# One-row and one-column products between the full products of a Fourier contraction, and unread products at a layer boundary

## The chip, the cores and the metric

The kernel runs on one core of one Trainium2 chip. A core has a matrix engine (PE, called TensorE), a vector engine (DVE), a scalar engine (ACT), GpSimd (POOL) and a queue engine (SP) that issues most DMAs. They share an SBUF of 128 partitions, and PE writes to eight banks of PSUM, which the other engines empty. The metric is device time in microseconds, the median of the runs shown; lower is better.

## The reference

Two kinds of layer alternate, A B A B, each added to its input after a layer norm. A is a Fourier mixing of 2048 rows by 512 columns; B is causal attention over four segments with a memory carried from segment to segment. Only A is touched by the change.

```python
def _A_ref(x, dft_seq_re, dft_seq_im, dft_hid_re, dft_hid_im):
    a = jnp.einsum("bsd,ed->bse", x, dft_hid_re)
    b = jnp.einsum("bsd,ed->bse", x, dft_hid_im)
    y = jnp.einsum("ts,bse->bte", dft_seq_re, a) - jnp.einsum("ts,bse->bte", dft_seq_im, b)
    return y
...
x = A_x
x = x + _A_ref(_layernorm(x, axis=-1), ...)
x = x + _B_ref(_layernorm(x, axis=-1), B_wq, B_wk, B_wv, B_wo, B_beta)
x = x + _A_ref(_layernorm(x, axis=-1), ...)
x = x + _B_ref(_layernorm(x, axis=-1), B_wq, B_wk, B_wv, B_wo, B_beta)
```

## The kernel before

The Fourier matrices hold cosines and sines, so their rows repeat with changed signs. The kernel folds the normalised input into eighths of the 2048 rows (octants), 128 rows to a tile and `k` = 0, 1 for the two tiles of an octant, and forms sums and differences of the octants on DVE. Then it contracts over the folded rows on PE. It runs this Fourier stage twice. What follows calls them Fourier layer 1 (at the start) and Fourier layer 2 (behind the first attention layer; there the argument `late` of `place_folded` is set, and its last octant comes straight from the attention's output projection).

The contraction, `contract(ps)`, runs for two halves `ps` = 0, 1 of the output. Each fills eight `u` tiles, four to a `kind` (0 for the cosine part, 1 for the sine part), one for each 128 of the 512 hidden columns (`d`). Its steps are:

- `odd(ps, kind, k)`: for two tiles of folded rows (`re` and `B`, which the trace names `hre` and `hAB`; in layer 2 both are `hAB`), four products of 128 rows by 256 columns each, into the odd columns of `u`.
- `even(ps, kind, k)`: for the tiles `S01` and `S32` (both `hS` in the trace), two sets of four products of 128 columns. Two families of small products hang on it. **One-row products**: for kind 0, `k` = 0, second set, a product whose operands `row["x"]` and `row["c", ps]` have a single row (`rows` in the trace), 128 columns, one after each of the four. **One-column products**: for `ps` = 0, kind 1, a column that is worked out for itself, `u[:, 0:1]`, gets a product of 128 rows and one column (`cmid,hS`), and for `k` = 0 also one of one row and one column (`cmid,rows`).

For `ps` = 0 the steps run in the order odd 0, odd 1, even 0, even 1 for `k` = 0, and again for `k` = 1. For `ps` = 1 they run kind by kind. After the last step of a kind, `drain` copies the four `u` tiles out (ACT, lines 576 and 577, then DVE, lines 594 to 602) into `vf`, and `hidden(j)` multiplies these along the hidden dimension: two `yi` products, and three `yr` products of which the middle one has a single row (`rows,wrap`). The steps of `contract(1)` and the first `hidden` units are interleaved by slot numbers given to `place`.

What sets the order: every engine runs its instructions in the order in which they were issued. `place` sorts generators into numbered slots, and the code of one slot is run after the code of the one before; PE's products are kept in exactly that program order (`keep_in_program_order`), while a scheduler may move instructions of DVE, ACT and SP among themselves by priority. The engines wait for one another through semaphores. The `u`, `yi`, `yr`, `po` and most other PSUM tiles come from one pool of seven banks (`bank`); an eighth holds `u` of kind 1, `d` = 3 (and later `pv_bank`).

The DVE operations that PE waits for in these stages are `fold_re` (line 426 where `k` = 0 and the tile is the first, line 428 otherwise), `fold_im` (lines 433 and 435) and `fold_even` (lines 440 to 454). In layer 2 the last octant is taken in by lines 380 to 388, behind the attention's last `po` products. `chk` (line 736, ACT) are activations over the given Fourier matrices that test their symmetry; they lie in the free time of ACT, and their loads in SP's queue.

Of the kernel before, what the change touches and what calls it, by code (L numbers as in the profile page):

```python
# [18 lines left out]
P = 128  # L19
# [39 lines left out]
def spectral_infini_kernel(  # L59
# [14 lines left out]
    V, A, G, T = nc.vector, nc.scalar, nc.gpsimd, nc.tensor  # L74
# [6 lines left out]
    def in_order(engine, name):  # L81
        op = getattr(engine, name)

        def call(*args, **kwargs):
            return tc.keep_in_program_order(op(*args, **kwargs))  # L85

        return call

    T = SimpleNamespace(matmul=in_order(T, "matmul"), transpose=in_order(T, "transpose"))
# [30 lines left out]
    def bank(name, shape=(P, 512), dtype=F32):  # L120
        return psum.tile(list(shape), dtype, name=name, tag="bank", bufs=7)
# [197 lines left out]
    def place_folded(x_in, x_out, t0, fold_at, folds=None, late=None):  # L319
        h = {}  # L320
        cf, vf, row, mid = {}, {}, {}, {}
        rest, minus = folded.masks

        def quad(w, k):
            if w == "re" and late is not None:
                w = "A"
            if w in "AB":
                if "xT" not in h:
                    h["xT"] = sb.tile([P, 2, 2, 2, 512], F32, name="hAB", tag="xT", bufs=1)
                return h["xT"][:, k, "AB".index(w)]  # L330
            if (w, k) not in h:
                tag = "ut" if w in ("C", "D32", "re") else "wd"
                h[w, k] = pair(f"h{w}", tag, 8, F32)
            return h[w, k]
# [189 lines left out]
        def bank4(ps, kind):  # L524
            if (ps, kind) not in banks:
                banks[ps, kind] = [
                    psum.tile([P, 512], F32, name="u", tag="pv", bufs=1)
                    if (ps, kind, d) == (0, 1, DT - 1)
                    else bank(f"u{d}")
                    for d in range(DT)  # L530
                ]
            return banks[ps, kind]

        def mm(out, lhsT, rhs, start=False, stop=False):
            T.matmul(out, lhsT, rhs, start=start, stop=stop, skip_group_check=True)

        def odd(ps, kind, k):
            for n, ab in enumerate((0, 1) if late is None else (1, 0)):
                for d, u in enumerate(bank4(ps, kind)):
                    mm(  # L540
                        u.rearrange("p (x o) -> p x o", o=2)[:, :, 1],
                        quad(("re", "B")[kind], k)[:, ab, d * P : (d + 1) * P],
                        cf[ps, k][:, ab, kind * 256 : (kind + 1) * 256],
                        start=(k, n) == (0, 0),
                        stop=(k, n) == (1, 1),
                    )

        def even(ps, kind, k):
            src = quad(("S01", "S32")[kind], k)
            for n, r in enumerate((2, 0)):  # L550
                for d, u in enumerate(bank4(ps, kind)):
                    dst = u.rearrange("p (x o) -> p x o", o=4)[:, :, r]
                    at = kind * 256 + n * P
                    mm(
                        dst,
                        src[:, n, d * P : (d + 1) * P],
                        cf[ps, 2][:, k, at : at + P],
                        stop=k == 1,
                    )
                    if (kind, n, k) == (0, 1, 0):  # L560
                        mm(dst, row["x"][:, d * P : (d + 1) * P], row["c", ps])
            if (ps, kind) == (0, 1):
                src = quad("S01", k)
                for d, u in enumerate(bank4(ps, kind)):
                    cols = slice(d * P, (d + 1) * P)
                    mm(u[:, 0:1], src[:, 1, cols], row["mid"][:, k : k + 1], stop=k == 1)
                    if k == 0:
                        mm(u[:, 0:1], row["x"][:, cols], row["mid"][0:1, 2:3])

        def drain(ps, kind):  # L570
            u = banks.pop((ps, kind))
# [36 lines left out]
            for to, of in pairs:  # L608
                G.tensor_copy(f[:, kind, :, to], v[:, :, of])
                if kind == 0:  # L610
                    G.tensor_copy(w[:, to], b[0:1, of])

        def contract(ps):
            if ps == 0:
                steps = [(f, kind, k) for k in range(2) for f in (odd, even) for kind in range(2)]
            else:
                steps = [(f, kind, k) for kind in range(2) for k in range(2) for f in (odd, even)]
            for f, kind, k in steps:
                f(ps, kind, k)
                if (f, k) == (even, 1):  # L620
                    drain(ps, kind)
                yield
# [79 lines left out]
        for ps in range(2):  # L702
            for n in (0, 2, 1):
                at = t0 + 8 + n if ps else t0 - 6 + n if late is not None else t0 - 10 + 3 * n // 2
                place(3.5, load_c(ps, n), [at])
        place(2, contract(0), [t0 + k for k in (0, 2, 4, 5, 6, 8, 9, 11)])
        place(2, contract(1), [t0 + k for k in (13, 14, 17, 19, 21, 22, 23, 24)])
        place(3.5, load_w(), [t0 + 9])
        for j in range(8):
# [684 lines left out]
    else:  # L1394
# [11 lines left out]
        for t, (edge, other) in zip(folded.masks, ((0.0, 1.0), (0.0, -1.0))):  # L1406
            V.memset(t, other)
            V.memset(t[0:1], edge)
        place_folded(
            Rows(x), mids[0], a1,  # L1410
            lambda k: [a1 - 12 + 3 * k, a1 - 6 + 4 * k, a1 - 4 + 4 * k, a1 - 2 + 4 * k],
# [5 lines left out]
        )  # L1417
        e = b1 + LB
        place_folded(
            mids[1], mids[2], a2,  # L1420
            lambda k: [e - 56 + 6 * k, e - 52 + 6 * k, e - 46 + 6 * k, e - 16 + 14 * k, e - 13 + 13 * k, e - 10 + 13 * k, e + 1 + 4 * k, *((e + 11, e + 13, e + 14) if k == 0 else (e + 15, e + 15, e + 17))],
            late=taken,
# [60 lines left out]
    ident = ident_b = mask = same_head = gate = None  # L1483
# [147 lines left out]
```

## Time and profile before

| | us |
|---|---|
| median of three runs | 1254.58 |
| lowest, highest | 1246.12, 1265.04 |
| the profiled execution | 1254.79 |
| its span, first to last instruction | 1252.9 |
| PE busy in it | 1148.4 (92%) |
| DVE busy | 962.3 (77%) |
| ACT busy | 845.8 (68%) |
| POOL busy | 440.3 (35%) |
| mean granted PE clock, of 1 | 0.968 |

Fourier layer 1 lies at about 0 to 130 us of the span and Fourier layer 2 at about 600 to 750, each overlapping the attention layer next to it. A busy share is a mean over stages that have different limits; in each stage the chain of waits tells which engine the end hangs on. The granted clock is that of PE: at 0.5 the array takes half of the clock pulses. The profile's PE busy time includes weight loads that a product waits for.

### The profile page before, as it was taken

How to read it: one execution, taken by the hardware profiler on the slowest of the kernel's cores; microseconds unless marked ns; L12 is line 12 of the kernel's file. 1: busy time of each engine (PE TensorE's matmuls, PEld its weight loads, DVE VectorE, ACT ScalarE, POOL GpSimd, SP SyncE). 2: the span in 40 equal slices, each digit the busy share in tenths (PEclk: the TensorE clock that was granted, in tenths of full speed). 3: DMA queues.
4: the chain of work that ended last, by engine and by line, in shares of the span. 5: the costliest groups of instructions: out<-in, count | busy, mean ns of one | idle time of the engine just before them, and what ended most of it. 6: DMA issues, size and time to landing. Idle time of an engine off the chain costs nothing.

```text
span 1252.9 us, 24306 instructions
## 1 busy us (share of the span) xinstructions
PE 1148.4 (92%) x7590; PEld 742.4 (59%) x7590; DVE 962.3 (77%) x3565; ACT 845.8 (68%) x1902; POOL 440.3 (35%) x774
## 2 busy tenths in 40 slices
PE   2999898999999999988889898899999999999887
PEld 2877464666655665544568765556666656655454
DVE  8878977778877777777695889867787778767872
ACT  2733487887787787786525426878777887878762
POOL 1121543534444444441110234444434544435200
PEclk9889998999999999998988999999999999999999
DMA  7877543435544454372426864434454444534511
GB/s 286 278 250 240 183 131 121 148 120 166 160 149 121 139 175 139 122 220 86 165 86 225 283 214 157 147 112 125 131 170 155 135 145 141 162 129 129 163 44 54
DMA packets 111125, 197.65 MB, mean 158 GB/s; under 512 B 13917, under 2 KB 63075, under 8 KB 110986
## 3 DMA queue, kind: packets, MB, share of 16 engines
q1 hardware_dynamic: 107722, 195.22, 48.2%
q8 instruction: 62, 1.02, 0.3%
q10 hardware_dynamic: 3264, 0.79, 0.3%
q14 instruction: 77, 0.63, 0.2%
HBM read 128.04 MB, written 67.14 MB: 156 GB/s over the span
## 4 chain that ended last, share of the span: by engine, by line
PE 64%; DVE 17%; ACT 7%; issue 5%; DMA 5%; POOL 2%; ACTq 0%; SPq 0%; DVEq 0%; POOLq 0%
PE pqk L85 11%; PE pv_bank L85 9%; PE sT L85 8%; PE nat L85 8%; DVE junk L934 7%; PE u L85 6%; PE po L85 5%; PE pvv L85 5%; DMA chk<-in_chk 3%; PE yr L85 2%; ACT pT L1008 2%; PE pm L85 2%; PE pM L85 2%; PE on L85 1%; ACT sT L1007 1%
## 5 line engine op out<-in xcount | busy, mean ns | idle before, releaser
L934 DVE CUSTOM_DVE_ANT_0 junk<-nat,mask 128x512 bf16<-128x512 f32 (+3 forms) x1024 | 499.9, 488 | 146.5 <-PE nat L85 113.0
L1008 ACT ACTIVATE pT<-sT 128x512 f32<-128x512 f32 x640 | 367.4, 598 | 44.5 <-PE sT L85 19.6
L1013 POOL TENSOR_SCALAR_AFFINE_SELECT pT<-pT 128x512 f32<-128x512 f32 x392 | 170.1, 447 | 404.7 <-ACT pT L1008 366.6
L85 PE MATMUL sT<-stkq,stkk 99*128 99x256 bf16 (+3 forms) x1024 | 250.6, 308 | 11.8 <-DVE mx L934 7.2
L85 PE MATMUL nat<-stkk,stkq 96*128 96x512 bf16 (+3 forms) x1024 | 237.8, 304 | 19.1 <-DVE mx L934 17.5
L1007 ACT ACTIVATE sT<-sT 128x256 f32<-128x256 f32 (+1 forms) x560 | 182.1, 334 | 52.4 <-PE sT L85 49.0
L85 PEld LDWEIGHTS <-stkk 99*128 99x128 bf16 x1024 | 83.1, 99 | 136.5 <-issue 122.2
L85 PE MATMUL pv_bank<-pT,vt 128*17 128x512 f32 (+3 forms) x2048 | 152.9, 437 | 0.0
L85 PEld LDWEIGHTS <-stkq 96*128 96x128 bf16 x1024 | 93.0, 99 | 65.2 <-issue 29.1
L85 PE MATMUL pqk<-xT,wq 128*128 128x512 f32 x384 | 127.6, 445 | 3.1 <-ACT xT L97 2.3
L85 PE MATMUL pqk<-xT,wk 128*128 128x512 f32 x384 | 126.3, 441 | 0.7 <-DVE mx L934 0.4
L85 PE MATMUL pvv<-wv,xT 128*128 128x512 f32 x384 | 124.2, 438 | 2.1 <-DVE mx L934 2.0
L85 PE MATMUL po<-wo,oh 128*128 128x512 f32 x384 | 122.5, 437 | 2.4 <-DVE oh L99 1.6
L736 ACT ACTIVATE chk<-chk,reps 128x1024 f32<-128x1024 f32 (+1 forms) x80 | 81.5, 1021 | 57.2 <-DMA chk<-in_chk 56.2
L85 PEld LDWEIGHTS pv_bank<-pT,vt 128*17 128x17 f32 x2048 | 53.5, 98 | 81.0 <-issue 76.7
L1118 POOL TENSOR_TENSOR onat<-onat,otmp 128x128 f32<-128x128 f32 x96 | 48.7, 514 | 104.3 <-DVE otmp L1117 101.0
L934 DVE DVE_READ_ACCUMULATOR2_ANT mx<- 128x1 f32 x1024 | 84.0, 82 | 0.0
L874 POOL TENSOR_TENSOR parts<-rem,parts 128x512 bf16<-128x512 f32 x60 | 71.8, 1196 | 27.8 <-ACT parts L870 24.2
L85 PEld LDWEIGHTS po<-wo,oh 128*128 128x128 f32 x384 | 68.4, 193 | 22.0 <-DVE oh L99 4.6
L85 PEld LDWEIGHTS pqk<-xT,wq 128*128 128x128 f32 x384 | 69.8, 193 | 16.4 <-ACT xT L97 2.8
L85 PEld LDWEIGHTS pvv<-wv,xT 128*128 128x128 f32 x384 | 68.6, 192 | 15.9 <-DVE mx L934 4.4
L85 PEld LDWEIGHTS pqk<-xT,wk 128*128 128x128 f32 x384 | 68.7, 194 | 13.4 <-issue 0.9
(216 smaller groups left out, 1679.4 us busy)
## 6 DMA issues: line engine op xcount, KB each, us to landing
chk<-in_chk SPq DMA_DIRECT2D x68, 512.0 KB
stkq<-scrq SPq DMA_DIRECT2D x64, 384.0 KB
stkk<-scrk SPq DMA_DIRECT2D x64, 384.0 KB
scrq<-parts SPq DMA_DIRECT2D x32, 384.0 KB
scrk<-parts SPq DMA_DIRECT2D x32, 384.0 KB
mid<-xrm SPq DMA_DIRECT2D x32, 256.0 KB
scrq<-parts SPq DMA_DIRECT2D x32, 256.0 KB
scrk<-parts SPq DMA_DIRECT2D x32, 256.0 KB
```

Source lines behind the costliest of these rows:

```text
L85: return tc.keep_in_program_order(op(*args, **kwargs))
L736: A.activation(t[:, c : c + row], t[:, c : c + row], AF.Abs, bias=rep[:, col : col + 1], scale=scale, accum_out=acc[:, col : col + 1],)
L874: E.tensor_tensor(out=parts[:, 2], in0=rem, in1=parts[:, 1], op=ALU.subtract)
L934: V.tensor_tensor_reduce(junk[:, :n], src, mask[:, 512 - n :], 1.0, 3e38, ALU.add, ALU.min, dst,)
L1007: A.activation(blocks, blocks, AF.Relu)
L1008: A.activation(dst, ps, AF.Exp, scale=-SCALE)
L1013: G.affine_select(blocks, blocks, pattern=[[0, n] for n in blocks.shape[1:-1]] + [[1, P]], compare_op=ALU.is_ge, fill=0.0, base=0, channel ...
L1118: G.tensor_tensor(out=dst, in0=dst, in1=tmp, op=ALU.add)
```

## The change

Three things change, all in `place_folded`.

- The one-row products of both contractions, and for `ps` = 0 the one-column products of `k` = 0, are no longer issued in `even`. They go into a list, `extras`, and `odd` takes them from there for `k` = 1: for `ps` = 0 one after each of its products, for `ps` = 1 one after every second.
- The one-column products of `k` = 1 stay where they were.
- In layer 2 alone (`late is not None`), `contract(0)` first issues fifteen products of the identity with itself, 128 by 128 in four-byte data, into a PSUM tile `warm` that nobody reads.

```diff
+        extras = []
+
         def odd(ps, kind, k):
...
                         stop=(k, n) == (1, 1),
                     )
+                    if k and extras and (ps == 0 or d % 2):
+                        mm(*extras.pop(0))
...
                     if (kind, n, k) == (0, 1, 0):
-                        mm(dst, row["x"][:, d * P : (d + 1) * P], row["c", ps])
+                        extras.append((dst, row["x"][:, d * P : (d + 1) * P], row["c", ps]))
...
                     cols = slice(d * P, (d + 1) * P)
-                    mm(u[:, 0:1], src[:, 1, cols], row["mid"][:, k : k + 1], stop=k == 1)
                     if k == 0:
-                        mm(u[:, 0:1], row["x"][:, cols], row["mid"][0:1, 2:3])
+                        extras.append((u[:, 0:1], src[:, 1, cols], row["mid"][:, 0:1]))
+                        extras.append((u[:, 0:1], row["x"][:, cols], row["mid"][0:1, 2:3]))
+                    else:
+                        mm(u[:, 0:1], src[:, 1, cols], row["mid"][:, 1:2], stop=True)
...
+        def warm(n):
+
+            ps = bank("warm")
+            for _ in range(n):
+                T.matmul(ps[:, :P], ident, ident, start=True, stop=True)
+
         def contract(ps):
...
+            if ps == 0 and late is not None:
+                warm(15)
```

On PE, in Fourier layer 1, at the turn from `k` = 0 to `k` = 1 of the first contraction, this stood before (a row gives the line, the operation, out<-in and the size of the output):

```order
L85 MATMUL u_283<-cmid,hS_184 128x1
L85 MATMUL u_283<-cmid,rows 128x1
L85 MATMUL u<-cmid,hS_184 128x1
L85 MATMUL u<-cmid,rows 128x1
L85 MATMUL u_229<-cf,hre 128x256
L85 MATMUL u_230<-cf,hre 128x256
L85 MATMUL u_231<-cf,hre 128x256
```

The last three rows are the first products of `k` = 1, which wait for DVE's line 428. On the same engine, the same products of `k` = 1 now, from the third of them on:

```order
L85 MATMUL u_231<-cf,hre 128x256
L85 MATMUL u_231<-rows 128x128
L85 MATMUL u_232<-cf,hre 128x256
L85 MATMUL u_232<-rows 128x128
L85 MATMUL u_229<-cf,hre 128x256
L85 MATMUL u_281<-cmid,hS_184 128x1
L85 MATMUL u_230<-cf,hre 128x256
L85 MATMUL u_281<-cmid,rows 128x1
L85 MATMUL u_231<-cf,hre 128x256
L85 MATMUL u_282<-cmid,hS_184 128x1
```

The four one-row and eight one-column products have moved from ahead of that wait to behind it, one after each of twelve full products.

On PE, in Fourier layer 1, in the second contraction (`ps` = 1), ahead of the first `hidden` unit, this stood before:

```order
L85 MATMUL u_496<-rows 128x128
L85 MATMUL u_497<-cf,hS_184 128x128
L85 MATMUL u_497<-rows 128x128
L85 MATMUL u_498<-cf,hS_184 128x128
L85 MATMUL u_498<-rows 128x128
L85 MATMUL yi<-wf,vf 128x256 x2
```

Now, on PE, behind the second `hidden` unit:

```order
L85 MATMUL u_495<-cf,hre 128x256
L85 MATMUL u_496<-cf,hre 128x256
L85 MATMUL u_495<-rows 128x128
L85 MATMUL u_497<-cf,hre 128x256
L85 MATMUL u_498<-cf,hre 128x256
L85 MATMUL u_496<-rows 128x128
L85 MATMUL u_495<-cf,hre 128x256
```

The four one-row products have moved from between products of 128 columns to behind every second product of 256 columns, past two `hidden` units. Fourier layer 2 changes in the same way in both places.

On PE, at the boundary of the first attention layer and Fourier layer 2 (with the semaphores that a row waits for), before:

```order
L85 MATMUL po<-wo,oh 128x512 [waits DVE_49]
L85 MATMUL po<-wo,oh 128x512 x9
L85 MATMUL u_8530<-cf,hAB 128x256 [waits DMAHW7_49,DVE_49,PE_49]
L85 MATMUL u_8531<-cf,hAB 128x256 [waits PE_49]
L85 MATMUL u_8532<-cf,hAB 128x256
L85 MATMUL u_8533<-cf,hAB 128x256
L85 MATMUL u_8530<-cf,hAB 128x256 [waits DVE_49]
```

And now:

```order
L85 MATMUL po<-wo,oh 128x512 [waits DVE_49]
L85 MATMUL po<-wo,oh 128x512 x9
L85 MATMUL warm<-ident 128x128 [waits PE_49]
L85 MATMUL warm<-ident 128x128 x14
L85 MATMUL u_8546<-cf,hAB 128x256 [waits DMAHW7_49,DVE_49,PE_49]
L85 MATMUL u_8547<-cf,hAB 128x256
L85 MATMUL u_8548<-cf,hAB 128x256
L85 MATMUL u_8549<-cf,hAB 128x256 [waits PE_49]
L85 MATMUL u_8546<-cf,hAB 128x256 [waits DVE_49]
```

The fifteen unread products stand between the attention's last projection and the first `u` product, which still waits for DVE and for its DMA.

On ACT, in Fourier layer 2, where the first rows of the next attention layer are prepared, before:

```order
L736 ACTIVATE chk,acc<-chk,reps 128x1024 [waits DMAHW2_49,Activation_49]
L97 ACTIVATE xT<-xnT 128x4x128 [waits PE_49]
L97 ACTIVATE xT<-xnT 128x4x128
L577 ACTIVATE ub<-u_8913 128x512 [waits PE_49]
L97 ACTIVATE xT<-xnT 128x4x128 [waits PE_49]
L576 ACTIVATE ua<-u_8912 128x512 [waits DVE_49]
L97 ACTIVATE xT<-xnT 128x4x128 [waits PE_49]
```

And now (lines 582 and 583 are lines 576 and 577 of before, and 750 is 736):

```order
L97 ACTIVATE xT<-xnT 128x4x128 [waits PE_49]
L97 ACTIVATE xT<-xnT 128x4x128
L583 ACTIVATE ub<-u_8929 128x512 [waits PE_49]
L750 ACTIVATE chk,acc<-chk,reps 128x1024 [waits DMAHW2_49,Activation_49]
L97 ACTIVATE xT<-xnT 128x4x128 [waits PE_49] x2
L582 ACTIVATE ua<-u_8928 128x512 [waits DVE_49]
```

One check has moved from ahead of the four copies `xT` to between them, and the copy `ua` behind them.

## The prediction

> **What bounds the kernel now.** I read the page's head and its chain of work, then the chain in order of time, then PE's timeline in the two Fourier stages, and last the windows, because the clock column told where PE was slow without waiting.
>
> ```profile
> span 1252.9 us, 24306 instructions
> PE 64%; DVE 17%; ACT 7%; issue 5%; DMA 5%; POOL 2%; ACTq 0%; SPq 0%; DVEq 0%; POOLq 0%
> ...
> 43.28 21.73 PE u L85 x112
> ...
> 647.48 35.38 PE u L85 x192
> ```
>
> PE carries 64% of the chain. The last two rows (start, us, what) are the `u` products of the contractions in Fourier layer 1 (from 43.28) and Fourier layer 2 (from 647.48): both lie on the chain, so a microsecond of PE there is a microsecond of the end. The profiled execution took 1254.79 us with this span, 0.2 above the median 1254.58; I sum against 1254.79.
>
> PE's timeline follows (start, us, then the group). Products of four-byte data appear as two records, so x32 is 16 products.
>
> ```profile
> 33.42 0.48 PE L85 MATMUL u<-rows 1*128 1x128 f32 x2
> ...
> 35.91 0.48 PE L85 MATMUL u<-rows 1*128 1x128 f32 x2
> ...
> 38.22 0.28 PE L85 MATMUL u<-cmid,hS 128*128 128x1 f32 x2
> ...
> 40.29 0.38 PE L85 MATMUL u<-cmid,rows 1*128 1x1 f32 x2
> 43.28 6.33 PE L85 MATMUL u<-cf,hre 128*128 128x256 f32 x16 [2.62 <-DVE hre L428]
> ...
> 52.91 3.73 PE L85 MATMUL u<-cf,hS 128*128 128x128 f32 x32
> 56.48 0.95 PE L85 MATMUL u<-cmid,hS 128*128 128x1 f32 x8
> 57.29 3.70 PE L85 MATMUL u<-cf,hre 128*128 128x256 f32 x16
> ...
> 64.94 1.40 PE L85 MATMUL yi<-wf,vf 128*128 128x256 f32 x4
> ...
> 73.38 3.62 PE L85 MATMUL u<-cf,hre 128*128 128x256 f32 x16
> 76.83 1.03 PE L85 MATMUL yi<-wf,vf 128*128 128x256 f32 x4
> 77.70 0.59 PE L85 MATMUL yr<-wf,vf 128*128 128x256 f32 x2
> 78.22 0.69 PE L85 MATMUL yr<-rows,wrap 1*128 1x256 f32 x2
> 78.84 0.70 PE L85 MATMUL yr<-wf,vf 128*128 128x256 f32 x2
> 79.38 1.95 PE L85 MATMUL u<-cf,hS 128*128 128x128 f32 x16
> ```
>
> Prices at full clock, from starts: a 256-column product 0.431 (73.38 to 76.83, eight), a 128-column one 0.223 (52.91 to 56.48, sixteen). In the one-row stretch a product starts every 0.415 (33.42 to 35.91, six steps), though a 128-column stream is 0.223: each switch between 128 rows and one row shows a weight load of 0.19. The one-column products start every 0.296 (38.22 to 40.29, seven steps). The same switch beside 256 columns: the three `yr` products, the middle one of one row, take 1.68 (77.70 to 79.38) against 3 x 0.431, so two switches cost 0.39 there too. Long neighbours do not hide them.
>
> The windows (us, busy per engine, granted clock, DMA) stand on a grid of 3.413 us on which the clock is exactly 0.50 or 1.00:
>
> ```profile
> core 0: us, PE busy (x) PEld busy (x) DVE busy (x) ACT busy (x) POOL busy (x), PEclk, DMA share, GB/s
> 45.19:48.61 3.42, 3.42 (x10) 2.70 (x9) 3.42 (x5) 1.47 (x4) 0.00 (x0) 0.50 0.70 238
> ...
> 62.26:65.67 3.41, 3.41 (x17) 2.51 (x17) 0.48 (x1) 2.29 (x5) 0.35 (x3) 1.00 0.87 348
> 65.67:69.09 3.42, 3.42 (x8) 1.89 (x7) 1.28 (x2) 1.66 (x4) 0.00 (x0) 0.50 0.02 6
> 69.09:72.50 3.41, 3.41 (x8) 2.29 (x8) 2.55 (x5) 0.00 (x0) 0.00 (x0) 0.50 0.43 153
> ...
> 642.53:645.94 3.41, 2.38 (x6) 1.97 (x7) 3.41 (x11) 0.00 (x0) 0.30 (x1) 0.50 0.41 121
> 645.94:649.35 3.41, 3.24 (x9) 2.07 (x8) 3.41 (x5) 0.63 (x1) 1.22 (x2) 0.50 0.29 114
> ...
> 659.59:663.01 3.42, 3.42 (x23) 3.21 (x22) 3.39 (x5) 2.16 (x3) 0.00 (x0) 1.00 0.71 204
> 663.01:666.42 3.41, 3.41 (x9) 2.70 (x8) 1.12 (x2) 1.56 (x4) 0.00 (x0) 0.50 0.79 261
> 703.97:707.38 3.41, 2.15 (x10) 1.94 (x11) 3.12 (x14) 2.19 (x3) 1.04 (x2) 1.00 0.76 297
> ```
>
> The clock falls after a window with little full-row streaming, even when PE shows busy all of it. 62.26 to 65.67 is mostly one-row pairs (full-row share 0.223/0.83 = 27%; with the `yi` behind them some 42%), and 659.59 to 663.01 is mostly one-column products (some 28%): both are followed by 0.50. The window 703.97, busy 63%, is not. So the fall lies between 42 and 63%. For the way back: 642.53 (70% busy) does not release, 645.94 (95%) does; `yi` and `yr` together (4 x 0.431 of 2.55 = 68%) fail in one window and release in the next. The edge is near 70%.
>
> The Trainium skill, "TensorE: Matmul & The Clock Gate", Part 1: The HAM clock gate, says that the window is free-running and about 3.4 us, and the gate half or full; the rows above agree. The same page, Why this matters for your kernels, asks only that PE have no idle gap over about 3 us; the full window 659.59 with its fall behind it disagrees, and the measurement decides. By that rule alone nothing but idle time would move the clock, and the estimate would be +4.4 us.
>
> **The change, part by part.**
>
> *Layer 1, first contraction.* Four one-row products (0.61 each: 0.223 and two switches) and eight one-column products (0.296) ran before 40.67 and so in the shadow of PE's wait for DVE, which ends at 43.28 whatever PE does. Now they run behind it: 4 x 0.61 + 8 x 0.296 = **+4.8**. Bounds: 1.7 if their weights loaded unseen, 4.8 by the rows; I take the rows.
>
> *The clock there.* At 43.28 it is half, as before. Before, sixteen plain products filled the window 45.19 and it came back at 48.61. Now the share is 0.431/1.04 = 41% beside one-row products and 0.431/0.727 = 59% beside one-column ones, both below 70%, so it stays until the last four plain products. Half clock runs at 0.51 of full: 64.94 to 73.38 is 8.44 for what takes 2 x 2.55 = 5.10 at full, with 6.83 of it at half. The 9.98 us of interleaved work then take 19.6, to 62.9, and the next grid line is 65.67: 22.4 us at half lose 11.0. Before, 9.63 for 16 x 0.431 lost 2.7. **+8.3**; bounds 0 (release at 48.61) and 8.3. The one-column share is nearest to the windows that failed, so I take 8.3.
>
> *Layer 1, second contraction.* The one-row pairs leave the place ahead of `yi`; the clock should not fall at 65.67: 8.44 - 5.10 = **-3.3**. Their four products cost the same 0.61 in the later place, two 256-column products to each (0.862/1.47 = 59%, inside 42 to 63, so a fall is possible but not likely). `yi` also waits for DVE's `vf`; the plain products ahead of it leave that little slack, bound 0 to 0.5, taken as 0.
>
> *Layer 2, the boundary.*
>
> ```profile
> 631.31 8.74 PE L85 MATMUL po<-wo,oh 128*128 128x512 f32 x36
> 643.56 3.75 PE L85 MATMUL u<-cf,hAB 128*128 128x256 f32 x8 [3.50 <-issue]
> 647.48 6.36 PE L85 MATMUL u<-cf,hAB 128*128 128x256 f32 x24 [0.17 <-DVE hAB L426]
> 653.67 1.28 PE L85 MATMUL u<-cf,hS 128*128 128x128 f32 x10
> ...
> 662.05 8.86 PE L85 MATMUL u<-cf,hAB 128*128 128x256 f32 x32
> 670.75 3.73 PE L85 MATMUL u<-cf,hS 128*128 128x128 f32 x32
> ...
> 682.78 1.43 PE L85 MATMUL yi<-wf,vf 128*128 128x256 f32 x4
> ...
> 691.22 3.62 PE L85 MATMUL u<-cf,hAB 128*128 128x256 f32 x16
> ```
>
> Fifteen unread products take 15 x 0.223 = 3.35, and the wait is 3.50 (640.05 to 643.56): they fit, delay nothing, and keep the clock. Four products then end at 645.3, but the next four need DVE's L426, ready at 647.48: PE waits 2.2 us instead. Only the twelve after that gain: 647.48 + 12 x 0.431 = 652.66 against 653.67, **-1.0**. If that 2.2 us gap falls whole into one window its share is 35% and a window at half costs 3.41 x 0.49 = 1.7; on the present grid it is split, so 0. The unread tile takes one PSUM bank of the rotation; PE alone is waited for, so nothing.
>
> *Layer 2, contractions.* The one-column stretch no longer empties a window: 670.75 - 662.05 = 8.70 against 16 x 0.431 = 6.90, **-1.8**. The one-row pairs leave the place ahead of 682.78: again 8.44 - 5.10, **-3.3**. The moved products cost as much as before, 0.
>
> *The other queues.* ACT's order shifts: a check now stands between the copies `ub` and the last two `xT`.
>
> ```profile
> 713.09 1.15 ACT L736 ACTIVATE chk<-chk,reps 128x1024 f32<-128x1024 f32 x1
> ...
> 715.20 0.59 ACT L577 ACTIVATE ub<-u 128x512 f32<-128x512 f32 x1
> ...
> 716.98 0.60 ACT L97 ACTIVATE xT<-xnT 128x512 fp32r<-128x512 f32 x1
> ```
>
> From 715.8 a check (1.15 and its read) ends at about 717.1, two copies at 718.2 instead of 717.6: **+0.6**, and `pqk` waits for them. SP's check loads and DVE's small statistics trade places; their cover is the contraction's PE time, and I cost them at 0.
>
> Sum: 4.8 + 8.3 - 3.3 - 1.0 - 1.8 - 3.3 + 0.6 = +4.3, so 1259.
>
> **Rivals.**
> *Layer 2 falls too.* Its one-row stretch, 4 x 1.04 us at 41%, is longer than a window; what follows is at 59%. If one window catches it, about 659.6, the remaining 6.6 us of mixed work run at half until plain products fill a window, some 17 us, losing 17 x 0.49 = 8.3: 1267. For it: 41% is under 42. Against: the grid must fit.
>
> *Layer 1 recovers at 48.61.* If one-row streams count for the gate, 8.3 becomes 0 and the time is 1251. For it: the release edge rests on few windows. Against: window 62.26 streamed, one-row products counted, well over half the time and still fell.
>
> *Weights hide beside long products.* Then 0.39 vanishes for each one-row product, 1.55 in each of the four places, and some 1.5 for the one-column ones in each layer; shares rise, and the 8.3 shrinks to about 3: 4.3 - 6.2 - 3.0 - 5.3, about 1245. Against: the `yr` rows. The Trainium skill, same page, Part 2: What happens when you issue a matmul, says that a weight load is pulled ahead when row groups do not conflict or the spare weight buffer is free; by that the estimate would be this one, and the `yr` rows do not bear it out.
>
> *Slower by over 2%.* The clock stays at half through both column stages, not only the mixed stretches. 25 us need 25/0.49 = 51 us more at half, fifteen windows. Against: plain stretches such as 52.91 to 56.48 fill whole windows.
>
> *The change does not do what it says.* The unread products, whose operand is the identity, do not hold the clock: only the 1.0 is lost, 1260.
>
> **How the numbers follow.** The sum's case 0.45 (1259, the last rival within it), layer 2 falling too 0.21 (1267), early recovery 0.16 (1251), hidden weights 0.10 (1245), others 0.08. The time told is the first. The runs before lie between 1246 and 1265, so the median itself moves by several us. The range 1247 to 1268 takes in the first three and leaves out the fourth and the tails. Faster or slower counts from 2%, 25 us, about what a measurement of this kernel can tell from no change. No case but the fourth rival reaches it: faster 0.01, same 0.96, slower 0.03.
>
> **What would show it.** Right: in layer 1 PE idle from about 36 (40.67 less the 4.8 moved) to 43.28, and the clock at 0.50 over five to seven windows from there; in layer 2 fifteen `warm` products ahead of 643.5, clock 1.00 at the first `u`, a gap of about 2 us before L426's product; clock 1.00 over the first two `yi` of each layer; one-row products at 0.6 beside 256 columns. Wrong: the clock back at 1.00 by 52 in layer 1; one-row products that add 0.25 or less; a half-clock stretch over layer 2's mixed products; or the late hidden stage waiting for DVE, so that PE's gain is not handed on.

## The result, and the profile after

| | before | after |
|---|---|---|
| median, us (20 runs each) | 1253.05 | 1260.76 |
| lowest, highest | 1246.12, 1265.04 | 1256.77, 1265.59 |
| the profiled execution | 1254.79 | 1259.06 |
| its span | 1252.9 | 1257.3 |
| mean granted PE clock | 0.968 | 0.975 |

The ratio is 1.0068, with a 95% interval of 1.0057 to 1.0080: about 8.5 us slower (0.0068 x 1253), less than 2%. The forecast was 1259. The mean clock went up while the time went up, so the profile must be read by stage.

The head of the page of the changed kernel, then rows of its chain of work in order of time (start, us, what):

```profile
span 1257.3 us, 24369 instructions
PE 60%; DVE 17%; ACT 8%; DMA 7%; issue 5%; POOL 2%; ACTq 0%; SPq 0%; DVEq 0%; POOLq 0%
...
43.38 32.16 PE u L85 x128
...
653.94 31.13 PE u L85 x184
```

In layer 1 the `u` products ahead of the first `hidden` unit are 32.16 us of the chain where they were 21.73. In layer 2 they are 31.13 where they were 35.38: one stage lost, the other gained.

PE's timeline of the changed kernel in layer 1 (start, us, group, and in brackets the idle time before it and what ended it):

```profile
32.24 3.73 PE L85 MATMUL u<-cf,hS 128*128 128x128 f32 x32
43.38 1.22 PE L85 MATMUL u<-cf,hre 128*128 128x256 f32 x2 [7.40 <-DVE hre L428]
44.53 0.79 PE L85 MATMUL u<-rows 1*128 1x128 f32 x2
45.25 1.22 PE L85 MATMUL u<-cf,hre 128*128 128x256 f32 x2
...
62.66 3.17 PE L85 MATMUL u<-cf,hAB 128*128 128x256 f32 x8
65.67 3.73 PE L85 MATMUL u<-cf,hS 128*128 128x128 f32 x32
...
70.05 3.70 PE L85 MATMUL u<-cf,hre 128*128 128x256 f32 x16
...
75.37 1.03 PE L85 MATMUL yi<-wf,vf 128*128 128x256 f32 x4
...
80.47 1.03 PE L85 MATMUL u<-cf,hre 128*128 128x256 f32 x4
...
86.26 1.13 PE L85 MATMUL yi<-wf,vf 128*128 128x256 f32 x4
...
95.24 2.40 PE L85 MATMUL u<-cf,hAB 128*128 128x256 f32 x10 [0.53 <-DVE ve L144]
...
705.33 2.40 PE L85 MATMUL u<-cf,hAB 128*128 128x256 f32 x10 [1.09 <-DVE xrm L677]
```

The last row is the same place in layer 2. In the kernel before, the timeline had at these two places:

```profile
87.39 2.40 PE L85 MATMUL u<-cf,hAB 128*128 128x256 f32 x10 [2.22 <-DVE xrm L663]
...
705.23 2.40 PE L85 MATMUL u<-cf,hAB 128*128 128x256 f32 x10 [2.22 <-DVE rt L159]
```

PE now stands idle from 35.98 to 43.38, since nothing small is left to fill the wait, and then takes 22.29 us (43.38 to 65.67) for sixteen full products and twelve small ones. One pair of a full and a one-row product takes 1.87 us there. Two `hidden` units take 5.10 (75.37 to 80.47), where they took 8.44.

The windows of the same kernel on the clock's grid, three of layer 1 and two of layer 2's placed products:

```profile
44.57:47.98 3.41, 3.41 (x9) 1.96 (x8) 3.41 (x5) 1.20 (x2) 0.00 (x0) 0.50 0.50 157
61.63:65.04 3.41, 3.41 (x10) 2.44 (x9) 0.00 (x0) 0.00 (x0) 0.00 (x0) 0.50 0.00 0
65.04:68.45 3.41, 3.41 (x29) 3.33 (x28) 0.73 (x2) 1.47 (x3) 0.00 (x0) 0.99 0.47 135
...
662.37:665.79 3.42, 3.42 (x18) 2.11 (x16) 3.42 (x7) 0.38 (x1) 0.00 (x0) 1.00 0.74 283
665.79:669.20 3.41, 3.41 (x18) 2.39 (x17) 3.38 (x5) 2.11 (x4) 0.00 (x0) 1.00 0.66 223
```

In layer 1 seven windows pass at half, from about 41.15, still in PE's wait, to 65.04 (23.9 us). From 44.57 on PE shows busy all of every one of them and the clock is still 0.50. In layer 2 the same mixture, entered at full clock, stays at 1.00. The mixture did not lower the clock there; in layer 1 it failed to raise it.

PE's timeline of the changed kernel at the boundary and in layer 2:

```profile
637.76 8.75 PE L85 MATMUL po<-wo,oh 128*128 128x512 f32 x36
646.35 3.51 PE L85 MATMUL warm<-ident 128*128 128x128 f32 x30
650.01 1.97 PE L85 MATMUL u<-cf,hAB 128*128 128x256 f32 x8 [0.16 <-PE warm L85]
653.94 5.45 PE L85 MATMUL u<-cf,hAB 128*128 128x256 f32 x24 [1.96 <-DVE hAB L426]
659.22 3.73 PE L85 MATMUL u<-cf,hS 128*128 128x128 f32 x32
662.84 0.70 PE L85 MATMUL u<-cf,hAB 128*128 128x256 f32 x2
663.47 0.48 PE L85 MATMUL u<-rows 1*128 1x128 f32 x2
663.88 0.70 PE L85 MATMUL u<-cf,hAB 128*128 128x256 f32 x2
...
667.01 0.70 PE L85 MATMUL u<-cf,hAB 128*128 128x256 f32 x2
...
673.37 1.99 PE L85 MATMUL u<-cf,hAB 128*128 128x256 f32 x8
675.20 3.73 PE L85 MATMUL u<-cf,hS 128*128 128x128 f32 x32
...
684.91 1.03 PE L85 MATMUL yi<-wf,vf 128*128 128x256 f32 x4
...
690.01 1.03 PE L85 MATMUL u<-cf,hAB 128*128 128x256 f32 x4
```

The first four `u` products are quick now, and the time goes into a new wait of 1.96 for L426. A full and a one-row product take 1.04 here (662.84 to 663.88).

Set side by side, the two profiled executions show where the change's time came and went:

| the same work in both | before | after | difference |
|---|---|---|---|
| layer 1, second contraction starts | 57.29 | 70.05 | +12.8 |
| first `yi` | 64.94 | 75.37 | +10.4 |
| third `yi` | 76.83 | 86.26 | +9.4 |
| attention 1, `pqk` x11 | 101.29 | 108.78 | +7.5 |
| its last `po` x36 | 631.31 | 637.76 | +6.5 |
| layer 2, first `yi` | 682.78 | 684.91 | +2.1 |
| attention 2, `pqk` x11 | 718.36 | 718.81 | +0.5 |
| end of the span | 1252.9 | 1257.3 | +4.4 |

### The profile page after: what moved, and what is told of

It is laid out like the page before. It is cut to its first block, busy times and chain, and to the rows that moved or that the text cites. A ratio compares the mean times of both kernels' runs of the same rounds, so it can differ in the third digit from the quotient of the medians.

```text
span 1257.3 us, 24369 instructions
## 1 busy us (share of the span) xinstructions
PE 1145.7 (91%) x7620; PEld 737.9 (59%) x7620; DVE 963.3 (77%) x3565; ACT 844.3 (67%) x1902; POOL 439.6 (35%) x774
## 4 chain that ended last, share of the span: by engine, by line
PE 60%; DVE 17%; ACT 8%; DMA 7%; issue 5%; POOL 2%; ACTq 0%; SPq 0%; DVEq 0%; POOLq 0%
PE pqk L85 10%; PE pv_bank L85 9%; PE sT L85 8%; PE nat L85 7%; DVE junk L948 7%; PE u L85 7%; PE po L85 5%; PE pvv L85 5%; DMA chk<-in_chk 4%; ACT pT L1022 2%; PE pm L85 2%; PE pM L85 2%; ACT sT L1021 2%; PE on L85 2%; PE yr L85 1%
## 5 line engine op out<-in xcount | busy, mean ns | idle before, releaser
L85 PE MATMUL sT<-stkq,stkk 99*128 99x256 bf16 (+3 forms) x1024 | 248.0, 305 | 16.0 <-DVE mx L948 8.9
L85 PE MATMUL nat<-stkk,stkq 96*128 96x512 bf16 (+3 forms) x1024 | 235.2, 301 | 18.5 <-DVE mx L948 16.7
```

## The experiments

Twelve kernels were run, six to twelve times each, beside 25 to 35 runs of the kernel before on the same chip. Three questions: is the loss in layer 1 the clock or the moved products; does each other part give what the sum said; and is there a better place for the small products. Most kernels switch the parts through one function, put into the changed kernel:

```diff
+        def deferred(ps):
+            return <condition>
...
-                        extras.append((dst, row["x"][:, d * P : (d + 1) * P], row["c", ps]))
+                        one = (dst, row["x"][:, d * P : (d + 1) * P], row["c", ps])
+                        extras.append(one) if deferred(ps) else mm(*one)
```

and the same for the one-column products; with `True` it is the changed kernel. Below only the condition is given, and whether the unread products run. The results:

| kernel | median, us | ratio to before | 95% interval |
|---|---|---|---|
| l1_first | 1264.66 | 1.0088 | 1.0059 to 1.0117 |
| second | 1243.78 | 0.9921 | 0.9892 to 0.9950 |
| l2_first | 1251.33 | 0.9979 | 0.9958 to 0.9999 |
| warm_only | 1255.25 | 1.0024 | 0.9999 to 1.0050 |
| fill_l1 | 1251.98 | 1.0010 | 0.9984 to 1.0035 |
| keep_l1 | 1247.41 | 0.9973 | 0.9947 to 0.9998 |
| grouped | 1246.97 | 0.9964 | 0.9941 to 0.9987 |
| grouped_fill | 1246.33 | 0.9965 | 0.9941 to 0.9988 |
| after_nowarm | 1262.38 | 1.0067 | 1.0038 to 1.0096 |
| keep_nowarm | 1246.99 | 0.9948 | 0.9927 to 0.9969 |
| second_warm | 1247.44 | 0.9970 | 0.9948 to 0.9992 |
| grouped_nowarm | 1246.83 | 0.9947 | 0.9925 to 0.9969 |

**Only layer 1's first contraction (l1_first).**

```diff
+            return late is None and ps == 0
...
-            if ps == 0 and late is not None:
+            if ps == 0 and late is not None and False:
                 warm(15)
```

> Only layer 1's first contraction (ps = 0) interleaves its small products; the second contractions, layer 2 and the boundary are as before. Theory 1 (the small products leave the shadow of the wait for line 428, and their mixing keeps the clock at half): first contraction ends at about 70 in the span instead of 57.3, clock 0.50 from about 41 to 65, total slower by 8 to 13 us (ratio 1.006 to 1.010). Rival A (only the 4.8 us leave the shadow, the half clock being an accident of the grid): +5 us, 1.004. Rival B (the loss of the changed kernel comes from the layer boundary, from layer 2 or from the reordered checks): no change, 1.000.

Its ratio is 1.0088, 11 us (0.0088 x 1253). PE's timeline in layer 1:

```profile
43.11 1.22 PE L85 MATMUL u<-cf,hre 128*128 128x256 f32 x2 [7.40 <-DVE hre L428]
...
71.00 3.70 PE L85 MATMUL u<-cf,hre 128*128 128x256 f32 x16
...
78.65 1.13 PE L85 MATMUL yi<-wf,vf 128*128 128x256 f32 x4
...
83.85 3.62 PE L85 MATMUL u<-cf,hre 128*128 128x256 f32 x16
```

The same idle 7.40 and 27.9 us to the second contraction, against 14.0 before (43.28 to 57.29). This one edit carries the whole loss and more, as the first theory had it.

The last two rows show something else. The second contraction of this kernel has its one-row products where the kernel before has them, and yet its first two `hidden` units took 5.20 (78.65 to 83.85) and not 8.44: in this execution the clock did not fall there.

**Only the second contractions, in both layers, without the unread products (second).**

```diff
+            return ps == 1
```

> Only the one-row products of the second contractions (ps = 1), in both layers, stand behind every second 256-column product. Theory 1: clock 1.00 over the first two yi units in both layers, 8.4 us of them become 5.1, but only in executions whose grid of windows fell on the old one-row stretch; total 2 to 7 us faster (ratio 0.995 to 0.998). Rival: DVE's work on xrm paces the hidden units, so that PE's gain ends in waits: 0.999 to 1.001 with waits of PE on DVE about 3 us longer behind the units.

The ratio is 0.9921, some 10 us (by its interval 6.3 to 13.5), where the first theory had 2 to 7. PE's timeline in layer 1 and layer 2:

```profile
62.95 1.13 PE L85 MATMUL yi<-wf,vf 128*128 128x256 f32 x4 [0.36 <-POOL vf L617]
...
68.15 1.03 PE L85 MATMUL u<-cf,hre 128*128 128x256 f32 x4
...
83.25 2.40 PE L85 MATMUL u<-cf,hAB 128*128 128x256 f32 x10 [0.86 <-DVE ve L144]
...
693.04 2.40 PE L85 MATMUL u<-cf,hAB 128*128 128x256 f32 x10 [1.09 <-DVE xrm L684]
```

Two units take 5.20 in layer 1 (62.95 to 68.15) and 5.10 in layer 2 (672.61 to 677.71) in place of 8.44, as the sum said. The `vf` wait that the prediction bounded at 0.5 is 0.36. And the later wait of PE, 2.22 before, is 0.86 and 1.09: the four one-row products, moved to behind the units, now fill a part of it. The sum had not counted that.

**Only layer 2's first contraction, without the unread products (l2_first).**

```diff
+            return late is not None and ps == 0
```

> Only layer 2's first contraction interleaves its small products; no unread products. Theory 1: the one-column stretch no longer lowers the clock, 16 products of 256 columns without a half-clock window, local gain 0 to 1.8 us less 0.5 for the dearer one-column places: ratio 0.998 to 1.001. Rival: the mixed stretch lowers the clock as in layer 1: 6 to 8 us slower, 1.005 to 1.007.

Its ratio of 0.9979 is 2.6 us, at the edge of what its interval tells from nothing. The clock does not fall in its mixed stretch. Nor does it in the five other kernels that place products there (the changed kernel, fill_l1, keep_l1, after_nowarm, keep_nowarm): the rival "layer 2 falls too" did not happen in six profiled executions. In one of them its condition was met: in keep_nowarm a whole window lay in the one-row stretch (shown in the last section).

**Only the unread products (warm_only).**

```diff
+            return False
...
             if ps == 0 and late is not None:
                 warm(15)
```

> Only the fifteen unread products at the boundary. Theory 1: clock 1.00 when the first u product of layer 2 starts, then a wait of about 2 us for line 426; gain about 1 us, up to 2.7 where the clock would also have been lost in the next window: ratio 0.998 to 0.9995. Rival A: products of the identity do not hold the clock, 1.000. Rival B: they delay the first u product or a PSUM bank, 1.001 to 1.003.

The place looks as forecast, with the clock at 1.00 and a wait of 1.96 for L426, and yet the time is not shorter: 1.0024, rival B's ratio. Rival B's cause is not seen: the first `u` product starts 12.26 us behind the start of the last `po` group (631.16 to 643.42), where it was 12.25 before. This was taken up again below.

**The changed kernel, with layer 1's wait filled (fill_l1).** Forty-four products of a two-byte identity with zeros, added to `u`, run while PE waits for L428.

```diff
+        def fill(u, n):
+            for _ in range(n):
+                mm(u[:, :384], ident_b, mask[:, :384])
...
             for f, kind, k in steps:
+                if (ps, f, kind, k) == (0, odd, 0, 1) and late is None:
+                    fill(bank4(0, 0)[0], 44)
                 f(ps, kind, k)
```

> The changed kernel, and in layer 1 PE's empty wait ahead of line 428 (35.9 to 43.4 us) is filled with 44 products of the two-byte identity with zeros, 384 columns each, which add nothing to a u tile: some 7.0 us of full-row streaming, ended before the wait is. Theory 1 (the half clock, not the moved products, is the larger part of layer 1's loss): clock 1.00 at the first product behind the wait, mixed products at 1.04 and 0.8 us a pair as in layer 2, first contraction ends about 9 us earlier than in the changed kernel, total 1250 to 1256. Rival A (the switches or a wait carry the loss): 1260, as the changed kernel. Rival B (zeros do not count for the gate): clock 0.50 there and 1260.

PE's timeline, then two windows:

```profile
35.78 7.32 PE L85 MATMUL u<-mask,ident_b 128*128 128x384 bf16 x44
43.35 0.70 PE L85 MATMUL u<-cf,hre 128*128 128x256 f32 x2 [0.25 <-DVE hre L428]
...
55.72 3.73 PE L85 MATMUL u<-cf,hS 128*128 128x128 f32 x32
60.10 3.70 PE L85 MATMUL u<-cf,hre 128*128 128x256 f32 x16
```

```profile
43.35:46.76 3.41, 3.41 (x13) 2.05 (x14) 3.41 (x5) 2.44 (x4) 0.00 (x0) 1.00 0.39 103
46.76:50.18 3.42, 3.42 (x18) 2.40 (x17) 3.42 (x6) 1.45 (x3) 0.00 (x0) 1.00 0.96 383
```

This separates the two terms of layer 1. The products are the same and start at the same time; only the clock differs. They take 12.37 us (43.35 to 55.72) in place of 22.29, so half clock cost 9.9 us of this stage; the other 12.37 - 16 x 0.431 = 5.5 are the moved products. In the time of the whole kernel the ratio went from 1.0068 to 1.0010, 7.3 us, which with the intervals (some 0.0028 together, 3.5 us) is in keeping with 9.9.

**The changed kernel, with layer 1's first contraction as before and the unread products (keep_l1).**

```diff
+            return late is not None or ps == 1
```

> The changed kernel, but layer 1's first contraction leaves its small products where they were before, in the shadow of the wait for line 428. Theory 1: all of the change's loss lies there; the rest is its second-contraction part (1243.8 alone) with layer 2's first contraction and the unread products, each 0 to -2: 1240 to 1246, faster than both kernels. Rival (the unread products or layer 2's mixing cost something, as the run with the unread products alone, 1255.3, might say): 1246 to 1250.

0.9973: the harm is gone, but the gain is smaller than `second` alone had. Its 1247.4 lies in the rival's range.

**The small products grouped where they were (grouped, grouped_fill).** Nothing is placed between full products; each four one-row products run in a row behind their four 128-column products, and the one-column products are sorted by kind. The unread products stay. The second kernel also fills layer 1's wait, with 27 products.

```diff
                     if (kind, n, k) == (0, 1, 0):
-                        extras.append((dst, row["x"][:, d * P : (d + 1) * P], row["c", ps]))
+                        one = (dst, row["x"][:, d * P : (d + 1) * P], row["c", ps])
+                        group.append(one)
+            for one in group:
+                mm(*one)
```

> The kernel before with the unread products, and no interleaving: the four one-row products of a place stand in a row behind their full products, and the one-column products of full rows ahead of those of one row. Theory 1 (a switch between 128 rows and one row costs 0.19 us, and a place now has two instead of eight): each place shorter by 1.2 us, four times in all of which the first lies in layer 1's wait; the one-row stretch, 1.3 instead of 3.3 us, can no longer empty a window, so the clock stays 1.00 over the first yi units: 1241 to 1246. Rival (each one-row product pays its own weight load, whatever stands beside it): no gain from the order, 1251 to 1255.

> As the run grouped, and what is left of layer 1's wait ahead of line 428 is filled with 27 products of the two-byte identity with zeros, about 4.3 us, adding nothing to a u tile. Theory 1: clock 1.00 at 43.3 or one window earlier than 48.6, the sixteen 256-column products behind the wait take 6.9 to 8.3 instead of 9.6 us; 1.3 to 2.7 us below the run grouped. Rival (zeros do not count for the gate): equal to the run grouped.

PE's timeline of `grouped` ahead of layer 1's first unit:

```profile
62.94 1.15 PE L85 MATMUL u<-rows 1*128 1x128 f32 x8
64.02 1.13 PE L85 MATMUL yi<-wf,vf 128*128 128x256 f32 x4
...
69.22 3.62 PE L85 MATMUL u<-cf,hre 128*128 128x256 f32 x16
```

Four one-row products in a row take 1.08 from the first start to `yi` (62.94 to 64.02): 4 x 0.223 and one switch of 0.19. The other switch shows around them: the eight products ahead start at 61.06 and need 1.78 by themselves, and the two units take 5.20 where they take 5.10 without one-row products ahead. In all that is 2.96 - 1.78 + 0.10 = 1.28, so 0.32 each in place of 0.61: the two switches of each product were most of its price. The clock stays at 1.00 over both units (5.20). The ratio is 0.9964, and 1246.97 lies just above the first theory's 1241 to 1246 and far from the rival's 1251 to 1255, so grouping alone does what the change wanted in the second contraction, without harm in layer 1. Filling layer 1's wait removes the half clock at 43.3 as well: the sixteen products take 7.01 (43.42 to 50.43) in grouped_fill and 9.74 (43.40 to 53.14) in grouped. But 0.9965 shows no gain from it that the runs can tell, so the forecast of 1.3 to 2.7 us was met in the stage and not in the time.

**The same with and without the unread products.** `warm_only` and `keep_l1` had left open whether the unread products cost time. Four kernels turn them off or on, and nothing else: the changed kernel without them (after_nowarm), keep_l1 without (keep_nowarm), second with (second_warm), grouped without (grouped_nowarm).

```diff
-            if ps == 0 and late is not None:
+            if ps == 0 and late is not None and False:
                 warm(15)
```

> The changed kernel without its fifteen unread products at the boundary of attention layer 1 and Fourier layer 2; every placed product as in the changed kernel, which took 1260.8. Theory 1, the local reading: the unread products hold the clock and so save 1.0 to 2.6 us behind the boundary; without them PE's products after the last projection run at half clock for some 3 to 7 us again, and the time is 1262 to 1263, a ratio of about 1.008 to 1.010. Rival, from the run with the unread products alone (1.0024): they cost about 3 us somewhere later, and the time is about 1258, a ratio of 1.004. No effect that lasts: 1.007 within 0.001.

> Layer 1's first contraction as before, both second contractions and layer 2's first contraction as in the changed kernel, no unread products. With the unread products this took 1247.4 (0.9973). Theory 1: without them 1 to 2.6 us slower, 1248.5 to 1250, a ratio of 0.998 to 0.999. Rival, the unread products cost 3 us later: about 1244.5, a ratio of 0.995. Also by the sum of the parts measured alone (0.9921 for the second contractions, 0.9979 for layer 2's first): 0.990, 1240; if it is above 0.994 those parts do not add up.

> The two second contractions as in the changed kernel, plus the fifteen unread products; both first contractions as before. Without the unread products this took 1243.8 (0.9921). Theory 1: the unread products save 1 to 2.6 us, about 1242, a ratio of 0.990 to 0.991. Rival, they cost about 3 us: about 1247, a ratio of 0.9945. If neither ratio is hit and the clock windows of the attention layers differ, the difference is where the windows fall and not the products themselves.

> The four one-row products of each contraction in a row where they were, the one-column products by kind, nothing between full products, no unread products. With the unread products this took 1247.0 (0.9964). Theory 1: 1 to 2.6 us slower without them, 1248 to 1249.5, a ratio of 0.997 to 0.9985. Rival, the unread products cost about 3 us: about 1244, a ratio of 0.994. Local check in both: a group of four one-row products takes about 1.1 us, and the clock stays at 1.00 over the first two hidden units of each layer.

With them less without them, in ratio: +0.0001 (changed kernel), +0.0025 (keep), +0.0049 (second), +0.0017 (grouped), and +0.0024 for warm_only against before. No pair shows a saving; the mean is +0.0023, some 2.9 us. Each difference is uncertain by about 0.003 to 0.004, so only that of `second` stands clear of it. By the expectations the changed kernel showed no effect, keep and grouped came near the rival, and second_warm lay above the rival's 0.9945. The boundary of after_nowarm:

```profile
654.36 3.75 PE L85 MATMUL u<-cf,hAB 128*128 128x256 f32 x8 [3.51 <-issue]
658.28 6.30 PE L85 MATMUL u<-cf,hAB 128*128 128x256 f32 x24 [0.17 <-DVE hAB L426]
664.41 3.73 PE L85 MATMUL u<-cf,hS 128*128 128x128 f32 x32
```

Without them four products run at half clock and end just as L426 is ready; with them PE is early and waits 1.96. What is saved is only on the next twelve products: 6.13 (658.28 to 664.41) against 5.28 (653.94 to 659.22), 0.9 us. That saving hangs on the grid too: with the unread products the twelve took 5.28 or 5.29 in all the profiles, without them between 5.28 (l1_first, 658.88 to 664.16) and 6.97 (keep_nowarm, 639.65 to 646.62). Where the time goes that the ratios add on top is not settled. A place for it was looked for in the traces and not found: from `pqk` to the end of the span the kernels with unread products are longer than their partners in three pairs and shorter in two, by up to 4.4 us, which is more than the effect sought.

## Why the prediction was right, point by point

The time, 1260.76, lies 1.8 above the forecast 1259, within the range. The sum was +4.3, though, and the runs show +8.5, so each term is checked. Nine kernels have each of the four parts either in or out (the changed kernel, l1_first, second, l2_first, warm_only, keep_l1, keep_nowarm, second_warm, after_nowarm). One size per part, fitted to their nine ratios by least squares, with no term between parts:

| part | predicted, us | fitted, us |
|---|---|---|
| layer 1, first contraction | 4.8 + 8.3 = +13.1 | +12.9 |
| second contractions, both layers | -3.3 - 3.3 = -6.6 | -7.0 |
| layer 2, first contraction | -1.8 | +0.1 |
| unread products at the boundary | -1.0 | +3.1 |
| the check on ACT | +0.6 | (in the others) |
| sum | +4.3 | +9.1 |

Each fitted size is uncertain by about 4 us (95%, from the residuals, whose spread is 2.3 us). The two large terms come out near their forecasts. The two small ones came out higher, and by this fit the difference between 4.3 and 8.5 sits in them, without either being settled.

*Layer 1, first contraction: right.* The forecast put the end of the slow stretch at 65.67, 22.4 us behind the wait; it is 65.04, 21.7 behind it. The step to the second contraction was +12.8 against 13.1. That it is the clock is shown by fill_l1. The moved products cost 5.5 there against 4.8 forecast. Half clock cost 9.9; the kernel before had lost 2.7 to it already, so 7.2 are new against 8.3 forecast. The two errors, one up and one down, nearly cancel: 12.7. In the other two kernels with this part and no filling the clock stayed at half as well, for eight windows each (l1_first to 67.3, after_nowarm to 66.1). The rival "layer 1 recovers at 48.61" is refuted: five windows in a row that were full of such mixed work did not release. At half clock a full product is 0.431/0.51 = 0.845, so its share was 0.845/1.87 = 45% beside the one-row products, and 0.845/1.474 = 57% beside the one-column ones ((62.66 - 50.87)/8 = 1.474 for a pair).

*The second contractions: right in mechanism, the size in part luck.* 5.10 in place of 8.44 in both layers. But the forecast took 8.44 from one execution in which the clock fell in both layers, and the old order does not always lose it. Four profiled kernels have that order (before, l1_first, l2_first, warm_only), which makes eight places: the two units took 8.44 to 8.49 in four of them, 6.8 in two and 5.20 in two, on average 7.2. So the clock was worth some 2.1 in each layer, 4.3 in all, and not 6.6. What the sum did not have either is that PE's later wait shrinks, 2.22 to 0.53 in layer 1, and in layer 2 from 2.22 to 1.09, as the moved products take its place. That holds whether or not the clock fell: in the four kernels of the old order the wait is 2.0 to 2.2 in every place. In the profiled executions that is 2.8 us less delay by `pqk`, and 2.5 in `second`. An estimate from these rows is 4.3 + 2.5 = 6.8, near the forecast 6.6 and the fitted 7.0: a term too high and a term left out made up for each other.

*Prices.* The one-row product beside 256 columns cost 1.04 - 0.431 = 0.61, as forecast, so the rival "weights hide beside long products" is refuted. The Trainium skill, "TensorE: Matmul & The Clock Gate", Part 2: What happens when you issue a matmul, lets weight loads be pulled ahead of running products where row groups do not conflict or the spare buffer is free; between products of 128 rows and of one row the 0.61 does not bear it out, while among one-row products (1.08 for four, which leaves no more than the one switch of 0.19 beside the stream of 4 x 0.223) the measurement is in keeping with it. The one-column price was wrong: (673.37 - 667.01)/8 - 0.431 = 0.364 and not 0.296, 0.5 us on eight. It is a mean of two prices: the product of 128 rows adds 667.68 - 667.01 - 0.431 = 0.24, and that of one row, with a switch on either side, 668.60 - 667.68 - 0.431 = 0.49. "The moved products cost as much as before, 0" fails by that much.

*Layer 2, first contraction: the step that was mis-sized.* "The one-column stretch no longer empties a window: -1.8" took one profiled execution for the rule. Between the two profiled executions the stage from the first products of 128 columns to the second contraction became shorter by 1.1 (653.67 to 675.13 before, 659.22 to 679.59 after). In second_warm, where that stretch is as before, the sixteen products behind it take 7.01 (657.06 to 664.07) with the clock at 1.00:

```profile
657.06 7.17 PE L85 MATMUL u<-cf,hAB 128*128 128x256 f32 x32
664.07 3.73 PE L85 MATMUL u<-cf,hS 128*128 128x128 f32 x32
```

Of the five profiled kernels in which that stretch is as before, two lost the clock behind it (before and second, 8.70) and three did not (l1_first, warm_only and second_warm, 7.01). Whether the fall happens there hangs on where the grid lies, so its removal is worth some 0.7 on average, and the dearer one-column products take 0.5 back. In the time its size stays open: l2_first alone gave -2.6, the fit +0.1.

*The boundary: right in its place, unproven in the time.* Fifteen products fit into the wait, the clock is 1.00, the gap for L426 is 1.96 against 2.2 forecast. The twelve products behind L426 gained 0.9 against 1.0. The rival "unread products do not hold the clock" is refuted there. But no pair of kernels got faster by it, and the cause of that stays open.

*ACT.* `pqk` x1 waits 1.47 for its `xT` copy where it waited 1.23, and starts 0.34 later in the profile than before (717.97 against 717.63); forecast 0.6.

*The coincidence.* The two profiled executions differ by 1259.06 - 1254.79 = 4.3, the sum to the tenth. That is luck: the difference was down to 0.5 at `pqk` of attention 2, because two waits (2.8) and the first attention layer (1.0) gave some 4 us back, and grew to 4.4 in the second attention layer, in which the change touches no instruction. Attention stages move by that much between kernels: from the first to the last `mT` product (one for each attention unit) the second attention layer took 455.9 before, 460.5 in the changed kernel, and between 455.4 and 460.8 over all fourteen profiles. Runs of one kernel move too: among the thirty runs of the kernel before in the last round the mean granted clock went from 0.966 to 0.983, and the runs with a lower one took longer (correlation -0.81, some 6 us for each 0.01). The Trainium skill, same page, Part 1, says that the window is free-running, so that one kernel shows different counts of slow products from run to run; that fits the different places of the half-clock windows here, though each kernel was profiled once.

## What to carry to other kernels

Before you move work out of a wait, ask what the matrix engine's clock is when the wait ends: small products that nobody misses in a wait become dear behind it, and mixed in among full products they kept the clock at half for seven windows. Group products that need the same switch instead of spreading them: that took the price from 0.61 to 0.32 each and gave as much as the placing did. And do not take a term from where one profiled execution happened to lose the clock; ask in how many positions of the grid it would, and test it in several builds, because the builds here scatter by some 2.3 us around what their parts explain.

## What was not expected of the hardware

- Products of zeros hold the clock like any others: forty-four two-byte products of an identity with zeros, 7.32 us, left it at 1.00 (fill_l1), where 7.40 us of idle time left it at 0.50.
- The edge below which the clock falls is lower than the prediction's middle: the window 662.37 to 665.79 of the changed kernel, 0.47 us of plain products and then pairs of 0.431 in 1.04, comes to 49% and was followed by 1.00, as was the next, also about 49%. In keep_nowarm a window of the grid lay whole in the one-row pairs of layer 2 (the first row below; the second is the window behind it):

```profile
650.97:654.38 3.41, 3.41 (x15) 1.93 (x15) 3.38 (x4) 0.48 (x1) 0.00 (x0) 1.00 0.88 269
654.38:657.80 3.42, 3.42 (x18) 2.60 (x19) 1.92 (x4) 3.24 (x6) 0.00 (x0) 1.00 0.59 184
```

Its share is 0.431/1.04 = 41%, and the clock stayed at 1.00, where 42% by the same working fell in the kernel before. So the edge lies near 42%, and shares worked out like this place it no closer than that.
- The state remembers: the same mixture keeps full clock if it starts there (layer 2 in six kernels and layer 1 in fill_l1, shares of 0.431/1.04 = 41% and 0.431/0.795 = 54%) and keeps half clock if it starts there (layer 1, 45 and 57%). Between the two edges, fall and release, the clock stays what it was.
- The parts measured alone hardly add up: 1.0088 x 0.9921 x 0.9979 x 1.0024 gives 1.0011 for the changed kernel, which measured 1.0068, as far off as the four intervals together allow (some 0.0053). Why `second` alone is as fast as 0.9921 was not found; its neighbours with one harmless part more have 0.9948 and 0.9970.
